# Chunks 0 to 3 and the weight conversion in a written order, O3 in the next chunk, scans straight from the loads

## Chip, cores, metric

One Trainium2 chip, one NeuronCore of it. The metric is the device time of one execution in microseconds (us).

## What is computed

Three layers one after the other, on 4 sequences of 768 steps (3072 tokens of 320 numbers): a linear recurrence with 8 heads of 40, a dense MLP with ELU (the kernel and this text call it MoE1), and a mixture of 8 experts with a balanced gate (MoE2).

```python
# recurrence, for each batch and head: state is 40 x 40
for t in range(S):                       # S = 768
    y[t]  = r[t] @ state
    Sa    = state @ a[t]
    state = state * w[t] - outer(Sa, b[t]) + outer(v[t], k[t])
# MoE1: x is y as (3072, 320), w_in 320 x 2048, w_out 2048 x 320
h = x @ w_in
x = where(h > 0, h, exp(min(h, 0)) - 1) @ w_out
# MoE2: 8 experts, w1 320 x 1024, w2 1024 x 320; P from x @ w_gate,
#       exp, then 8 rounds of row and column normalisation
out = sum over e of P[:, e:e+1] * (relu(x @ w1[e]) @ w2[e])
```

## The kernel before

**The recurrence in chunks.** The 768 steps are cut into 24 chunks of 32. Within a chunk the steps are solved together for all 32 pairs of batch and head, by small matmuls and one triangular solve; the state Y goes from chunk to chunk. A chunk c consists of these pieces, each a function that is called by a token of an order list:

- `ldw`, `ldk`, `lu`, `lv`: loads on SP's queue of WA (w and a), KE (k and b), VU (v), and of rB and rO (r). Many tiles exist once (r1 pool), so a load waits for the last reader of the chunk before.
- `prep`: VectorE clamps w twice (L316, into `wr` reversed, L317, into `wq`), one scan for the products F (L320), a reciprocal, a second scan for xE (L326); GpSimd makes aE (L328) and multiplies KE twice by F (L337); ACT copies aE into aB. It is a generator of five steps.
- `E1`, `E2`: transposes of KE and xE on TensorE, each with an ACT copy. `E3`: matmuls of KE with aB, on VectorE a mask (L367, into Am), then four stores of Am to DRAM (Ad, L382). `LT`: Ad comes back in the layout of the solve (L390).
- `T`, in function `tsolve`: the triangular solve on VectorE, instruction pairs Tt and Wk (L420 and L422 with halves for chunks 0 to 5, 15 pairs; L429 and L436 after that, 31 pairs), for one or two chunks at a time. Then stores to DRAM (Td, L444) and loads back (TT, L448).
- `E4`: matmuls of Am with VU. `H1`: matmuls of aE with Yw (L465), and an ACT copy to RH. `H2`: matmuls of TT with RH (L494), ACT copies to VU; chunks 0 to 5 do it twice, with L484 and RH on VectorE (L485) between. `H3`: matmuls of KB with VU (L518), and Y on VectorE. `YW`: GpSimd makes Yw. `H4`: transposes of Yw, ACT copies to Ss. H1, H2, H3, YW are what one chunk waits for from the one before.
- `O1`: transposes of VU, copies to uE (ACT and VectorE). `O2`: matmuls with rB, a mask on VectorE (L367, into Gm). `O3a`: matmuls of rO with Ss (L566). `O3b`: matmuls with Gm (L577), on VectorE a product (L580), a GpSimd copy, and a store of the chunk's output to DRAM (yd). These use four PSUM banks in turn; O1 and O3 have banks 2 and 3, E2 and O2 bank 2, E3 and the transposes of xprep bank 3 (table "ps").

**MoE1 beside it.** A unit is one of 16 slices of the hidden size for one of 12 blocks of 256 tokens (two chunks): 8 matmuls (L620), two ACT steps (L622, L623), g on VectorE (L629), gh on ACT, gl on GpSimd (L633), and 8 matmuls (L647 to L651) two units later. A token `m` advances by half a unit; `x` and `xl` advance `xprep`, which transposes a block of outputs (L603) and splits it on ACT and VectorE (L608). Before units can run their weights must be converted: 32 conversions (`w_in_split`, `w_out_split`), each a load of 320 to 384 KB, three VectorE instructions on the bits (L204 to L206), one on ACT, two on GpSimd.

**Order.** From chunk 4 on (`"fixed": 4`) each engine but SP runs its instructions in the order in which the lists "order" and "order2" (chunks below 6) call them: `pin_since` ties each instruction to the one before it on its engine. A `+3` means the piece of chunk c+3; a token `p` advances a running solve by three instructions, `G` lets it begin to be pumped. For chunks 0 to 3 the list "start" gives the pieces of chunks 0 and 1 and some of 2 to 5, and the lists go on at c = 2; but there the order on each engine is chosen by the scheduler, by priorities. The conversions are called in three groups (`w_5`, `w_5`, `w_22`). The solves of chunks 2 and 3 run singly, in the tokens `u` and `t`. SP's queue is ordered by the scheduler throughout.

**MoE2.** After chunk 23 and the last units of MoE1, `phase_b` runs 8 experts over 6 blocks of 512 tokens, in units of 128 hidden columns: `mm1` (L856), a split on ACT and VectorE (L859, L860), `mm2` (L899 to L901), and at the end of a block an accumulation (L910). Weights are loaded 11 units ahead. A range check reads w again at its side, and the output is stored per 128 tokens.

## Time and profile before

| | us |
|---|---|
| median of 3 runs | 2272.39 |
| the runs | 2266.86 to 2277.91 |
| the profiled execution | 2277.48 |
| its span, first to last instruction | 2275.6 |
| TensorE busy | 2146.8 (94%) |
| VectorE busy | 947.0 (42%) |
| ACT busy | 808.4 (36%) |
| GpSimd busy | 469.5 (21%) |

The profile calls the engines PE (TensorE, with PEld for its weight loads), DVE (VectorE), ACT, POOL (GpSimd) and SP. A busy share is an average over the whole span; the rows below give it by stretch. PEclk is the granted TensorE clock as a share of full speed. A wait is the idle time of an engine just ahead of an instruction, with the work whose end is thought to have released it; where an instruction waits for several, the one that came last by the profile is named.

### The profile page before, as it was taken

The numbers are of one execution on the slowest core, as the hardware profiler recorded it, in microseconds if no ns is written. First come the engines' busy times: TensorE is split into PE (matmuls) and PEld (weight loads), VectorE is DVE, ScalarE is ACT, GpSimd is POOL, SyncE is SP. The second block draws the span as 40 slices with busy tenths as digits, with TensorE's granted clock in tenths as the row PEclk, the third lists the DMA queues.
The fourth block names the chain that finished last, engine by engine and source line by source line (L and its number), as shares of the span: only waits on it lengthen the run. The fifth ranks groups of instructions, "written<-read, shape, count | busy, mean of one in ns | idle before, by whom it ended". The sixth has DMA issues, their size and how long they took to land.

```text
span 2275.6 us, 48283 instructions
## 1 busy us (share of the span) xinstructions
PE 2146.8 (94%) x20483; PEld 1931.9 (85%) x20483; DVE 947.0 (42%) x1963; ACT 808.4 (36%) x1789; POOL 469.5 (21%) x553
## 2 busy tenths in 40 slices
PE   2478999999999999999999999999999999999998
PEld 2367889888898989898888888888888888888887
DVE  7774777766666622532222222222222222222222
ACT  2243455544555555323324324223223212112111
POOL 5442344434343244002002002002002002001000
PEclk9998899999999999999999999999999999999999
DMA  6544344334443232101002012002002001000000
GB/s 169 151 116 116 91 112 109 102 100 102 107 105 78 60 90 84 45 1 55 19 20 71 21 32 77 26 26 77 26 26 70 1 1 52 1 1 20 24 24 25
DMA packets 179234, 138.34 MB, mean 61 GB/s; under 512 B 103873, under 2 KB 152386, under 8 KB 179010
## 3 DMA queue, kind: packets, MB, share of 16 engines
q1 hardware_dynamic: 179010, 135.17, 21.5%
q8 instruction: 162, 2.65, 0.5%
q14 instruction: 62, 0.51, 0.1%
HBM read 116.63 MB, written 18.48 MB: 59 GB/s over the span
## 4 chain that ended last, share of the span: by engine, by line
PE 75%; DVE 10%; DMA 7%; SPq 3%; issue 2%; ACT 1%; POOL 1%; DVEq 0%; ACTq 0%; POOLq 0%
PE h L856 28%; PE pa L900 10%; PE pa L901 10%; PE pa L899 10%; PE ph L620 4%; PE h L845 2%; DVE Wk L436 2%; DMA LT<-Ad 2%; PE a L647 2%; DVE Tt L429 1%; DMA WA<-in_wa 1%; PE a L648 1%; PE a L649 1%; SPq L448 1%; DMA Ad<-Am 1%
## 5 line engine op out<-in xcount | busy, mean ns | idle before, releaser
L860 DVE SCALAR_TENSOR_TENSOR hl<-h,hh 128x512 fp32r<-128x512 f32 x384 | 265.2, 691 | 765.9 <-ACT hh L859 765.4
L859 ACT ACTIVATE hh<-h 128x512 fp32r<-128x512 f32 x384 | 229.3, 598 | 899.7 <-PE h L856 899.2
L856 PE MATMUL h<-xs,a 128*128 128x512 f32 x2280 | 546.8, 394 | 0.0
L856 PEld LDWEIGHTS h<-xs,a 128*128 128x128 f32 x2280 | 421.1, 188 | 109.1 <-issue 25.4
L899 PE MATMUL pa<-a,hh 128*128 128x320 f32 x1536 | 474.0, 309 | 1.8 <-ACT acc L906 1.6
L900 PE MATMUL pa<-a,hl 128*128 128x320 f32 x1536 | 475.4, 310 | 0.0
L901 PE MATMUL pa<-a,hh 128*128 128x320 f32 x1536 | 475.2, 309 | 0.0
L899 PEld LDWEIGHTS pa<-a,hh 128*128 128x128 f32 x1536 | 288.8, 188 | 7.1 <-ACT acc L906 1.8
L900 PEld LDWEIGHTS pa<-a,hl 128*128 128x128 f32 x1536 | 288.9, 188 | 5.0 <-issue 0.2
L901 PEld LDWEIGHTS pa<-a,hh 128*128 128x128 f32 x1536 | 289.0, 188 | 0.0
L807 POOL TENSOR_TENSOR a<-rw,a 128x384 fp32r<-128x384 f32 x64 | 65.4, 1022 | 1055.3 <-ACT a L805 1046.4
L633 POOL TENSOR_TENSOR gl<-g,gh 128x256 fp32r<-128x256 f32 x192 | 162.5, 846 | 410.6 <-ACT gh L631 296.0
L620 PE MATMUL ph<-X,Wt 128*128 128x256 f32 x1536 | 237.3, 299 | 0.6 <-DVE g L629 0.5
L620 PEld LDWEIGHTS ph<-X,Wt 128*128 128x128 f32 x1536 | 206.3, 199 | 5.1 <-DVE g L629 1.0
L910 DVE SCALAR_TENSOR_TENSOR acc<-pa,Pg,acc 128x320 f32<-128x320 f32 x168 | 80.9, 545 | 184.5 <-PE pa L901 184.5
L629 DVE SCALAR_TENSOR_TENSOR g<-m,ph 128x256 f32<-128x256 f32 x192 | 80.2, 418 | 181.3 <-ACT m L623 164.5
L622 ACT ACTIVATE m<-ph 128x256 f32<-128x256 f32 x192 | 73.5, 383 | 176.7 <-PE ph L620 168.6
L631 ACT ACTIVATE gh<-g 128x256 fp32r<-128x256 f32 x192 | 80.0, 417 | 124.9 <-DVE g L629 123.8
L436 DVE TENSOR_TENSOR Wk<-Wk,Tt 128x132 f32<-128x132 f32 (+24 forms) x279 | 119.2, 427 | 6.5
L856 PE MATMUL h<-X,a 128*128 128x512 f32 x456 | 109.1, 394 | 0.6 <-DVE X L608 0.6
L856 PEld LDWEIGHTS h<-X,a 128*128 128x128 f32 x456 | 84.0, 188 | 22.6 <-issue 5.0
L429 DVE TENSOR_TENSOR Tt<-Wk,LT 128x132 f32<-128x132 f32 (+24 forms) x279 | 92.2, 330 | 19.6 <-DMA LT<-Ad 11.7
(183 smaller groups left out, 2713.0 us busy)
## 6 DMA issues: line engine op xcount, KB each, us to landing
LT<-Ad SPq DMA_DIRECT2D x24, 512.0 KB
rw<-in_moe_w SPq DMA_DIRECT2D x64, 160.0 KB
WA<-in_wa SPq DMA_DIRECT2D x24, 416.0 KB
KE<-in_kb SPq DMA_DIRECT2D x24, 416.0 KB
...
```

The source lines that it names most:

```text
L429: V.tensor_tensor(out=tv, in0=Wk[:, :, 0:ni, j:j + 1].to_broadcast(sh), in1=LT2[:, :, j, j + 1:C].unsqueeze(2).to_broadcast(sh), op=ALU.mult,)
L436: dve["T"] = V.tensor_tensor(out=Wk[:, :, 0:ni, j + 1:C], in0=Wk[:, :, 0:ni, j + 1:C], in1=tv, op=ALU.subtract)
L620: T.matmul(ph, lhsT=Wt[0:kp, wi, 128 * f:128 * f + 128], rhs=X[0:kp, xi, :], start=(i == 0), stop=(i == 7))
L629: V.scalar_tensor_tensor(out=g, in0=m, scalar=-1.0, in1=ph, op0=ALU.add, op1=ALU.max)
L633: G.tensor_tensor(out=gl, in0=g, in1=gh.bitcast(F32), op=ALU.subtract)
L856: T.matmul(h, lhsT=a1[:, wi, :], rhs=X[bk][:, xi, :], start=(i == 0 and n == 8), stop=(i == n - 1), skip_group_check=(n == 7))
L859: dve["hh"] = A.activation(out=hh, in_=h, func=AF.Relu)
L860: V.scalar_tensor_tensor(out=hl, in0=h, scalar=0.0, in1=hh.bitcast(F32), op0=ALU.max, op1=ALU.subtract)
L899: T.matmul(o, lhsT=hh[:, ts_], rhs=a2[:, 0, :], start=(f == 0), stop=False)
L900: T.matmul(o, lhsT=hl[:, ts_], rhs=a2[:, 0, :], start=False, stop=False)
L901: T.matmul(o, lhsT=hh[:, ts_], rhs=a2[:, 1, :], start=False, stop=(f == NF2 - 1))
L910: V.scalar_tensor_tensor(out=at, in0=o, scalar=Pg[:, tt, e:e + 1], in1=at, op0=ALU.mult, op1=ALU.add)
```

## The change

It changes four things.

1. **Chunks 0 to 3 and the 32 conversions** get a written order on all engines but SP. The new list START holds their pieces one step at a time, with the conversions in three tokens (`d` load, `b` bits on VectorE, `o` ACT and GpSimd), 11 units of MoE1 (`m`), and the solves in pairs, chunks 2 and 3 together (`u` begins one, `s_10` runs ten steps). All of it is pinned. The lists "order" and "order2" now begin at c = 4. For chunks 0 and 1, aE and the products of KE move from GpSimd to VectorE. The LT tiles of chunks 2 and 3 and chunk 1's loads share a tile (`two`).
2. **O3a and O3b** of chunk c stand at the top of chunk c+1 (`+-1`), O3b's matmuls first, then E4, O3a, H1. Which of O3a and O3b starts and ends the accumulation is decided by which comes first.
3. **E3** of chunk c+3 stands behind H2 instead of ahead of H1; LT moves with it.
4. **The scans** read w from the loaded tile: the host puts a zero ahead of each row of 32, the first scan runs backwards over it. The two clamps and their tiles go; xE has rows of 33, so ACT copies it into a dense tile xC for the transposes of E2. The range check skips the zeros.

Besides, the last four units of MoE2 run their second matmuls for the first two token tiles of all four units, then for the other two.

```diff
+START = """
+lu_0 prep_0*5 E3_0 ldw_2 E3_0 LT_0 E1_0 E2_0 prep_1*5 E3_1*2 LT_1 ldk_2 E4_0 H1_0 E1_1 E2_1 lu_1 d*2 lv_0 b o u_0_1 d b o prep_2 d prep_2*2 ldw_3 b
+s_10 s_11 b prep_2 s_10 o d prep_2 E3_2 b o E3_2 LT_2 E2_2 ldk_3 H2_0 o E1_2 prep_3*2 d*2 H2_0 prep_3 H2_0 O1_0 H3_0 prep_3*2 E3_3 b H3_0 o O1_0 d
+E3_3 YW_1 ldw_4 b E4_1 LT_3 O2_0 H1_1 E1_3 prep_4 ldk_4 E2_3 u_2_3 b o d O2_0 s_10 O3b_0 d lu_2 o H2_1 O3a_0 O3b_0 s_10 H2_1 s_10 prep_4 H2_1 prep_4
+ldw_5 H3_1*2 b o d O1_1*2 H4_1 lv_1 YW_2 O2_1 E4_2 prep_4*2 E3_4 b O3a_1 d O2_1 o prep_5 H1_2 O3b_1 b E3_4 LT_4 o O3b_1 s_9 E1_4 ldk_5 xl E2_4 d
+prep_5 H2_2 prep_5 x*2 b x*2 H2_2 prep_5 m prep_5 o ldw_6 b o d m H2_2 d E3_5 b m E2_5 E3_5 H3_2*2 E1_5 ldk_6 o d O1_2 prep_6*2 lu_3 m O1_2 H4_2 YW_3
+E4_3 m b o d u_4_5 prep_6 H1_3 lv_2 b O2_2 ldw_7 m o O2_2 d LT_5 H2_3 b o d s_10 m H2_3 O3a_2 b o d m O3b_2*2 H2_3 prep_6*2 b prep_7 ldw_8 d o H3_3 m
+E3_6 H3_3 b o d m E3_6 E2_6 E1_6 ldk_7 m b d o LT_6 s_10 prep_7 O1_3 H4_3 lu_4 b YW_4 m d o O1_3 b o lv_3 O2_3 b o d m O2_3 prep_7 b o d m O3a_3 b
+O3b_3 s_20 d b o m d m prep_7 b m o prep_7 m*2 O3b_3 d m o d m x b o b d m x b d o*2 x*2 b o
+"""
...
-    "order": "T lv E4 m p E3+3 xl m E3+3 p H1 m p E2+3 LT+3 m p H2 lu+1 m prep+4 p E1+3 ldk+4 m prep+4 p x m prep+4 p H3 m G x H3 p O1 m O1 p H4 m YW+1 prep+4 p O2 ldw+5 x m O2 p m x p O3a m prep+4 p O3b m O3b p m p m p w",
+    "order": "T O3b+-1 E4 p O3a+-1 H1 lv m p O3b+-1 m lu+1 m p H2 E3+3 xl m E3+3 p p m p E2+3 LT+3 m prep+4 E1+3 ldk+4 m prep+4 p x m prep+4 p H3 m H3 G x p O1 m O1 p H4 m prep+4 YW+1 p O2 m ldw+5 x O2 p m x p m prep+4 p m p m p",
+    "order2": "T O3b+-1 E4 m p O3a+-1 H1 lv m O3b+-1 p xl m p H2 lu+1 m prep+4 p H2 m prep+4 p H2 E3+3 m E3+3 E2+3 LT+3 prep+4 p H3 E1+3 ldk+4 x x m G H3 p O1 m O1 p H4 m YW+1 prep+4 p O2 ldw+5 x m O2 p m x p m prep+4 p m p m p m p",
-    "start": "prep_0 E3_0 LT_0 prep_1 E3_1 LT_1 E1_0 E2_0 lu_0 E1_1 w_5 E2_1 lu_1 E4_0 H1_0 ld_2 prep_2 E3_2 LT_2 lv_0 E1_2 T_0_1 u_2 w_5 ld_3 E2_2 H2_0 t_2 u_3 H3_0 O1_0 O2_0 O3a_0 O3b_0 E4_1 YW_1 H1_1 H2_1 O1_1 w_22 lu_2 ld_4 prep_3 H4_1 lv_1 O2_1 O3a_1 O3b_1 xl H3_1 YW_2 E3_3 LT_3 t_3 E2_3 E1_3 prep_4 E3_4 LT_4 E2_4 E1_4 ld_5 prep_5 ldw_6",
+    "start": START,
...
-    "fixed": 4,
+    "queue": False,
...
+    ws = np.concatenate([np.zeros_like(e["w"][..., :1]), e["w"]], -1).reshape(N, 2, D, -1)
+    out["wa"] = lay(np.concatenate([ws, np.zeros_like(ws[..., :1]), e["a"].reshape(N, 2, D, -1)], -1))
...
-        V.tensor_scalar(out=wr[0:HR, :, 1:C + 1], in0=wv[:, :, ::-1], scalar1=WLO, scalar2=WHI, op0=ALU.max, op1=ALU.min)
-        V.tensor_scalar(out=wq[0:HR, :, 1:C], in0=wv[:, :, 0:C - 1], scalar1=WLO, scalar2=WHI, op0=ALU.max, op1=ALU.min)
+        V.tensor_tensor_scan(out=F[0:HR, 1:NW + 1][:, ::-1], data0=z.WA[0:HR, 1:NW + 1][:, ::-1], data1=flat(dr)[0:HR], initial=0.0, op0=ALU.mult, op1=ALU.add)
...
+        V.tensor_tensor_scan(out=flat(z.xE)[0:HR], data0=z.WA[0:HR, 0:NW], data1=flat(dq)[0:HR], initial=0.0, op0=ALU.mult, op1=ALU.add)
+        (V if c < 2 else G).tensor_tensor(out=z.aE[0:HR].rearrange("p g (b t) -> p (g b) t", t=C), in0=z.WA[0:HR, NW + 1:].rearrange("p (x t) -> p x t", t=C), in1=z.xE[0:HR, :, 0:C], op=ALU.mult)
...
+        A.copy(out=z.xC[0:HR].rearrange("p g (b t) -> p (g b) t", t=C), in_=z.xE[0:HR, :, 0:C])
...
+        s, z.begun = not hasattr(z, "begun"), True
...
-                SY.dma_start(out=raw[0:rows], in_=wa_d[x][:, 0:size] if n == "w" else wp_d[x] if n == "i" else wo_d[x * 128:(x + 1) * 128, :])
+                SY.dma_start(out=raw[0:rows], in_=wa_d[x][:, 0:NW].rearrange("p (x t) -> p x t", t=C + 1)[:, :, 1:] if n == "w" else wp_d[x] if n == "i" else wo_d[x * 128:(x + 1) * 128, :])
...
+                seq += [(mm2, x + (p,)) for p in (range(0, TB // 2), range(TB // 2, TB)) for x in u]
```

## Rows read from the trace of the kernel before

**Rows 1.** Busy us by stretch: PE, PEld, DVE, ACT, POOL; PEclk, DMA share, GB/s
```profile
0.00:126.00 126.00, 51.99 (x809) 42.27 (x809) 91.81 (x190) 33.84 (x72) 64.38 (x85) 1.00 0.57 158
...
126.00:217.00 91.00, 78.76 (x1316) 70.36 (x1317) 53.55 (x124) 36.69 (x88) 35.74 (x43) 0.87 0.47 120
...
217.00:290.00 73.00, 67.63 (x1230) 63.03 (x1227) 45.32 (x107) 33.32 (x82) 22.80 (x29) 0.86 0.33 84
...
290.00:800.00 510.00, 485.53 (x8482) 455.72 (x8482) 351.26 (x831) 263.96 (x673) 198.79 (x229) 0.97 0.38 97
...
905.00:2276.00 1371.00, 1361.80 (x7630) 1205.00 (x7629) 380.10 (x660) 379.02 (x722) 99.37 (x106) 1.00 0.10 32
```

**Rows 2.** Timeline, chunks 0 to 3: start, us, engine, line, operation, [idle before <-releaser]
```profile
25.88 1.98 PE L365 MATMUL P<-aB,KE 104*64 104x64 f32 x32 [0.18 <-ACT aB L453]
...
33.79 1.16 DVE L367 TENSOR_TENSOR Am<-P,cst 128x1024 f32<-128x1024 f32 x1
...
45.36 0.22 DVE L420 TENSOR_TENSOR Tt<-Wk,LT 128x60 f32<-128x60 f32 x1 [8.87 <-DMA WA<-in_wa]
...
67.69 1.93 PE L494 MATMUL P<-RH,TT 64*64 64x40 f32 x32
...
111.11 1.93 PE L494 MATMUL P<-RH,TT 64*64 64x40 f32 x32 [1.78 <-DVE RH L485]
...
163.35 1.13 PE L494 MATMUL P<-RH,TT 64*64 64x40 f32 x32
...
213.07 0.55 PE L398 MATMUL P<-VU,Am 128*64 128x40 f32 x12
```

**Rows 3.** Groups by line on DVE, 0 to 217 us: busy, mean ns | idle before
```profile
L205 DVE SCALAR_TENSOR_TENSOR tmp<-raw,tmp 128x384 int32<-128x384 int32 (+1 forms) x32 | 21.5, 675 | 0.5
...
L206 DVE SCALAR_TENSOR_TENSOR tmp<-raw,tmp 128x384 int32<-128x384 int32 (+1 forms) x32 | 20.1, 632 | 0.6
...
L420 DVE TENSOR_TENSOR Tt<-Wk,LT 128x48 f32<-128x48 f32 (+19 forms) x60 | 19.5, 325 | 22.4 <-DMA LT<-Ad 8.9 <-DMA WA<-in_wa 8.9 <-DMA Wk<-in_consts 3.4
...
L204 DVE TENSOR_SCALAR tmp<-raw 128x384 int32<-128x384 int32 (+1 forms) x32 | 12.5, 392 | 16.9 <-DMA raw<-in_wp 7.3 <-DMA raw<-in_moe_w_out 4.5 <-POOL yt L581 1.9
...
L320 DVE TENSOR_TENSOR_SCAN F<-wr,dr 104x528 f32<-104x528 f32 x8 | 9.9, 1246 | 0.0
...
L317 DVE TENSOR_SCALAR wq<-WA 104x496 f32<-104x496 f32 x8 | 3.8, 477 | 0.0
...
L316 DVE TENSOR_SCALAR wr<-WA 104x512 f32<-104x512 f32 x8 | 3.4, 423 | 6.1 <-DMA WA<-in_wa 6.1
```

**Rows 4.** Timeline of DVE, one conversion instruction of chunk 0's stretch
```profile
20.77 2.30 DVE L205 SCALAR_TENSOR_TENSOR tmp<-raw,tmp 128x384 int32<-128x384 int32 x1
```

**Rows 5.** Group of O3a on PE, 290 to 800 us; then timeline of chunk 7
```profile
L566 PE MATMUL P<-Ss,rO 40*32 40x40 f32 x1024 | 14.9, 206 | 19.4 <-ACT m L623 12.2 <-DVE X L608 6.5 <-ACT m L622 0.5
...
338.58 1.12 PE L620 MATMUL ph<-X,Wt 128*128 128x256 f32 x8
...
339.64 1.22 DVE L367 TENSOR_TENSOR Gm<-P,cst 128x1024 f32<-128x1024 f32 x1
...
340.96 0.78 PE L566 MATMUL P<-Ss,rO 40*32 40x40 f32 x64 [1.26 <-ACT m L623]
```

**Rows 6.** Busy us by stretch, columns as in the first group, in chunk 12
```profile
490.00:500.00 10.00, 8.33 (x123) 7.64 (x123) 6.66 (x19) 2.11 (x6) 4.04 (x5) 0.66 0.22 59
```

**Rows 7.** Timeline of SP's queue and DVE around one solve's end, chunks 9 and 10
```profile
402.40 4.94 SPq L444 DMA_DIRECT2D Td<-Wk  x6
...
407.56 1.91 SPq L448 DMA_DIRECT2D TT<-Td  x4
...
410.79 1.22 DVE L367 TENSOR_TENSOR Am<-P,cst 128x1024 f32<-128x1024 f32 x1 [1.94 <-DMA TT<-Td]
...
415.99 1.91 SPq L382 DMA_DIRECT2D Ad<-Am  x4
...
424.29 0.22 DVE L429 TENSOR_TENSOR Tt<-Wk,LT 128x62 f32<-128x62 f32 x1 [1.12 <-DMA LT<-Ad]
```

More of the change, by code (lines that the diff above doesn't have):

```diff
@@ new lines, in conv, with tokens @@
+            if i < len(wgen):
+                conv_load(*wgen[i]) if n == "d" else (conv_bits if n == "b" else conv_out)(convs[i])
+                cvn[n] += 1
+                if n == "o" and i + 1 == len(wgen):
+                    cvx.close()
+                    late.append(moe.enter_context(tc.tile_pool(name="late", bufs=1)))
+        def tokens(x):
+            for t in x.split():
+                t, k = (t + "*1").split("*")[:2]
+                yield from [t] * int(k)
+        first_ins = traced()[-1]
```

220 lines of the change are left out of this document (104 added, 116 removed), and 3 rows, old and new, of the table PLAN.

## The prediction

> **What bounds the kernel now.** I read the busy time by stretch first [rows 1]. From 905 us to the end TensorE is busy for 1361.8 of 1371 us at a granted clock of 1.00: the second mixture of experts (MoE2) is limited by TensorE alone, and the change touches only its last four units. Everything else lies before 905. From 0 to 126 us TensorE works for 52.0 us and VectorE for 91.8; from 126 to 217 they work for 78.8 and 53.6, at a mean clock of 0.87. At about 217 the chunk loop reaches chunk 4, whose first matmuls, E4, stand at 213.07 [rows 2]. From 290 to 800 TensorE is busy for 485.5 of 510 us at 0.97. So time can be won in two places: up to 217, where 86 us of TensorE are idle and a chain through all engines is the limit, and from 217 to 800, where TensorE is nearly full and some 30 us are idle, with a clock that falls now and then.
>
> The work is conserved. By the tokens of the order lists, before has finished 12 units of the first MoE when chunk 3 ends and after has finished 11; from then on both do the same number in each chunk (8 from chunk 5 on). So what is won early is won at the end too, less one unit: 16 matmuls of 256 columns, 1.9 us (eight stand in 1.12 us with the last one's drain [rows 5], 0.96 a half unit without it).
>
> **Part 1: chunks 0 to 3 in fixed order.** When does chunk 4's E4 start, before at 213.1? The steps of before [rows 2]: E3 of chunk 0 at 25.9, the solve of chunks 0 and 1 from 45.4, H2 of chunk 0 at 67.7, the second H2 of chunk 1 at 111.1, of chunk 2 at 163.4.
>
> *To the solve.* After, VectorE does two memsets fewer and then chunk 0 alone. WA lands near 5 us; then a scan of 1.25 [rows 3], a reciprocal, the other scan, aE and both KE products, which are now on VectorE (0.63 each, by the two-source L206 [rows 3], 1.9 together), with two ACT copies beside them: E3 of chunk 0 near 10, its mask done near 13. Chunk 1 repeats it, and its mask ends near 21, before at 35.0 [rows 2]. From there before takes 10.4 us until the solve starts (Ad store, LT load), so it starts near 31 instead of 45.4. Conversions and scans of chunk 2 (8 us) fill most of the wait.
>
> *To H2 of chunk 1.* From the start of the solve to H2 of chunk 0 before takes 22.3 us, of which some 3.5 are other VectorE work that now stands elsewhere: H2 near 50. Behind it VectorE waits for matmuls (8.6 us until RH, 5 us until Y); Y ends near 65, and H1 of chunk 1 near 71, behind E3 of chunk 3, E4 and O2. The next 20 solve steps (chunks 2 and 3 in one solve) stand ahead of chunk 1's RH on VectorE and wait for the LT of chunk 3, whose mask ends near 67: 67 + 10.4 = 78. RH is then ready near 85, and so is the second H2 of chunk 1 (before 111.1).
>
> *To chunk 4.* From chunk 1 to chunk 2 the second H2 takes before 52 us, to chunk 4's E4 another 50. After, H1 of chunk 2 stands behind E3 of chunk 4, which waits for GpSimd's KE products, near 104; the second H2 of chunk 2 is near 119, of chunk 3 near 153. Behind that VectorE still has 36 us of its list (13 conversions at 1.7, 30 solve steps, a mask, seven g): chunk 4 begins near 187.
>
> A second count for that end: VectorE is busy for 145.4 us up to 217 [rows 1]. The change takes away the two clamps of eight chunks (7.2 us), a quarter of the 120 solve instructions, since chunks 2 and 3 become one solve (60 are L420, 19.5 us: 9.7 with the others), and memsets (1), and adds 3.8 for chunks 0 and 1 [rows 3]: 131 us are left. My chain holds some 50 us of waits (31 up to 85 us, about 20 later): 181. I take 187, 26 us earlier, less 1.9 for the unit: **24 us**. Bounds: with half of these waits 156 (55 us); with all of before's 72 us of idle time 203 (8 us). The ACT copy from xE to xC is new, 0.4 to 0.7 us a chunk by the clamps of as many elements [rows 3], hidden: ACT is half idle, and E2 has units to spare; without that cover it costs up to 24 x 0.7 = 17 us. A reversed read cost the clamp L316 nothing against the forward L317 [rows 3]; a scan's reversed write is not in the trace: from nothing to a doubling, 1.25 us a chunk, hidden in the loop, up to 5 us here. I take nothing.
>
> A conversion costs VectorE 1.7 us (54.1 us for 32 [rows 3]). Single two-source instructions are long where GpSimd works: L205, 0.68 in the mean, took 2.30 at 20.77 [rows 4]. After, a conversion's bits often run beside the last one's GpSimd subtractions. If each of the 64 took 1.3, 42 us would be added; I take the mean of before, which holds such cases. The Trainium skill (GPSIMD Engine Reference, 1. Specifications) says that GpSimd's SBUF interfaces are shared with VectorE and contended by instructions with two SBUF inputs; the trace agrees. By that rule the denser start goes towards the 42 us, by the rows of before towards none.
>
> **Part 2: chunks 4 to 23.** From 290 to 800 TensorE idles for 19.4 us ahead of L566, O3a [rows 5]. The profile names ACT m and the X subtraction; but in chunk 7 the mask Gm runs from 339.64 to 340.86 and O3a starts at 340.96, after 1.26 us of idle time: O3a writes the bank that Gm reads, half a unit behind it, and in chunks with an xprep the bank that X reads too. After, O3b comes first, over three half units later at the top of the next chunk, and then O3a: Gm is done by then. I count 18.7 us, those named by m and X. E4 and H1 simply follow; Am, VU and Yw are made long before.
>
> The clock: behind such a wait in chunk 12 the granted clock is 0.66 from 490 to 500 us [rows 6]. At the lower level of 1.2 GHz for 6.8 of these 10 us, TensorE loses 3.4. The 510 us lose 0.03 x 510 = 15 in this way [rows 1], nearly all in four such places. I take 13.6; if the falls stay, 0.
>
> What is late next? E3 now stands behind H2, and H2 waits for TT. Before, in chunk 10: Td is issued at 402.40, right behind the solve; TT at 407.56; the mask ends at 412.0, but its Ad store is issued only at 415.99, behind SP's other transfers; the next solve starts at 424.29, waiting for LT [rows 7]: 21.9 us. After: TT there 9.3 us behind the solve (409.5 and 2 to land, an estimate), H2 1.1, E3 1.2, half a unit and the mask 2.2, Ad and LT 8.3: 22.1, about the same. The solve is spread over 20 half units and some 15 us of the chunks' own matmuls, 34.6. Together that is 57 us for a pair of chunks, while TensorE needs 32 x 0.96 + 2 x 14 = 59 (14 an estimate: what is left of a chunk). It holds, by 2 us. H2 before has eight half units and six groups of matmuls, about 13 us, between the solve's end and its turn; after six and four, 8.8 to 9.8: a wait of up to 1 us in each of nine pairs, 3 with a delayed Td. I take **minus 4 us** (0 to minus 27). The later yd store costs nothing in the loop (six half units ahead of its reader) and up to 2 us once, in the last chunk; I count it in that range.
>
> From 217 to 290, 5.4 us are idle and 0.14 x 73 = 10 are lost to the clock [rows 1], part of it behind O3a: **6 us** (0 to 15). Loop: 18.7 + 13.6 - 4 = **28 us** (8 to 33).
>
> **Part 3, the rest.** With the last group's second matmuls in two halves, two accumulations instead of four are left behind the last matmul: under 0.5 us. The range check reads w in rows of 128 bytes instead of 2 KB, 24 times, while the DMA engines are a tenth busy [rows 1] and weights are loaded 11 units ahead: nothing.
>
> **Sum.** 24 + 6 + 28 = 58 us off the profiled execution's 2277.5, whose span is 2275.6: 2219. That execution was near the slowest of the four (2266.9 to 2277.9); off the median of 2272.4 it gives 2214. I say **2216**, between them and nearer the median.
>
> **Rivals.** (a) *The start wins little* (0.15): a fixed order stalls at its first late operand, and VectorE has its 72 idle us again. Start 8, total 42: 2232. For it: one late LT holds VectorE's whole list. Against: before pays the same wait, 8.9 us of it [rows 3]. (b) *Contention in the start* (0.05): 64 two-source instructions at 1.3 us put chunk 4 at 229, start minus 18, total 16: 2257. For it: the 2.30. Against: the mean of 0.68. (c) *The loop keeps its period* (0.16): new waits for TT, or a clock that still falls, leave 8 us of the loop: 2236. For it: 9.3 against 8.8 to 9.8. (d) *The start is bound by the recurrence alone* (0.14): chunk 4 begins near 165: 2194. (e) *Slower* (0.05): the solve's loop through DMA becomes the limit. Place: SP's queue, where the mask's Ad stands behind loads that now wait longer (rO behind the later O3a, yt behind the later yd). Each us by which that delays Ad beyond 2 is lost in each of ten pairs; at 8 the gain is gone, at 10 it gives 2292. Before, the delay was 4 us and came from TT, which is issued by then. (f) *Nothing changes* (0.04), as the scheduler's order was as good: 2270.
>
> **How the numbers follow.** The forecast has 0.41. The range leaves out no more than 0.2: it reaches over (a), (c) and (d) with their bounds, 2188 to 2250. About 0.5% (11 us) is what a measurement of this kernel can tell from no change. Faster: the forecast and (a) to (d), some of (b) aside: 0.88. Same, with (f): 0.06. Slower: 0.06.
>
> **What would show it.** Right: E3 of chunk 0 near 10, the solve from 31, the second H2 of chunk 1 near 85, chunk 4 near 187; no idle time ahead of O3a or O3b, and a clock of 1.00 from 300 to 750. Wrong: chunk 4 after 205; TensorE waiting at H2 for TT, or VectorE for LT above 3 us a pair; dips of the clock in the old places.

## The result, and the profile after

The changed kernel takes 2243.67 us (median; 2241.65 to 2252.16), the kernel before, run beside it, 2273.93 (2266.86 to 2277.91): a ratio of 0.9877 with an interval of 0.9841 to 0.9914. That is 30 us less, where 58 were forecast, and it lies inside the forecast's range of 2188 to 2250. The profiled execution is the one of 2241.65, its span 2239.8.

Busy time by stretch of the changed kernel (columns as in [rows 1], which it answers):

```profile
0.00:126.00 126.00, 68.73 (x1308) 60.70 (x1309) 82.79 (x160) 41.89 (x92) 41.39 (x60) 0.84 0.59 156
126.00:217.00 91.00, 69.49 (x1149) 63.62 (x1147) 64.33 (x122) 38.65 (x95) 45.02 (x64) 0.77 0.51 139
217.00:290.00 73.00, 68.08 (x1204) 64.35 (x1203) 52.69 (x120) 39.22 (x98) 27.01 (x31) 0.95 0.42 106
290.00:800.00 510.00, 485.36 (x8718) 463.14 (x8717) 346.26 (x791) 274.12 (x700) 201.00 (x235) 0.98 0.37 94
905.00:2239.00 1334.00, 1328.85 (x7444) 1175.15 (x7442) 360.76 (x620) 364.52 (x699) 99.41 (x106) 1.00 0.11 30
```

The stretch of MoE2 is as full as it was. Up to 126 us TensorE does 68.7 us of work instead of 52.0. But from 290 to 800 it is busy for 485.4 of 510 us, against 485.5 in [rows 1]: the 24 idle us of the loop are all still there.

The timeline of the changed kernel at the steps of [rows 2] (start, us, engine, line, operation, idle time before and its releaser; L383 is E3, for other tiles also O2, L436 the solve, L510 H2, L416 E4; a row stops where the stretch that was asked for stops, so it can show fewer matmuls than the group has):

```profile
11.21 1.97 PE L383 MATMUL P<-aB,KE 104*64 104x64 f32 x32 [11.21 <-ACT aB L469]
...
31.94 0.22 DVE L436 TENSOR_TENSOR Tt<-Wk,LT 128x60 f32<-128x60 f32 x1
...
50.37 0.41 PE L510 MATMUL P<-RH,TT 64*64 64x40 f32 x2 [10.46 <-DMA TT<-Td]
...
84.70 0.55 PE L510 MATMUL P<-RH,TT 64*64 64x40 f32 x6 [8.00 <-DVE RH L501]
...
116.88 0.33 PE L510 MATMUL P<-RH,TT 64*64 64x40 f32 x2
...
143.46 0.36 PE L510 MATMUL P<-RH,TT 64*64 64x40 f32 x5
...
188.44 0.44 PE L416 MATMUL P<-VU,Am 128*64 128x40 f32 x4
```

E3 of chunk 0 stands at 11.2, the solve starts at 31.9 (45.4 in [rows 2]), H2 of chunk 0 is at 50.4 (67.7), the second H2 of chunk 1 at 84.7 (111.1), of chunk 2 at 116.9 (163.4), of chunk 3 at 143.5, and E4 of chunk 4 at 188.4 (213.1): 24.6 us earlier.

The group of O3a, 290 to 800 us, of the changed kernel (columns as in [rows 5]):

```profile
L583 PE MATMUL P<-Ss,rO 40*32 40x40 f32 x1152 | 14.3, 200 | 0.0
```

Its 19.4 us of idle time [rows 5] are gone. In their place, in the view of TensorE's waits over the same stretch (what waited, for whom: us in all, times, longest):

```profile
PE P L383 <- issue: 5.7, 4, 1.7
PE P L481 <- issue: 5.7, 6, 1.6
PE P L365 <- ACT xT L469: 4.1, 6, 0.9
PE P L510 <- DMA TT<-Td: 2.5, 7, 0.7
PE ph L638 <- DVE g L647: 1.8, 6, 0.5
```

E3 (L383) and H1 (L481) wait, E1 (L365) waits for a copy of ACT, H2 for TT, MoE1 for g. "issue" means that the view names no releaser. Together with some smaller ones that makes 24.6 us again. From E4 of chunk 6 to E4 of chunk 23 the changed kernel takes 511.3 us, the profiled execution of before 521.6. Those 10 us and the start's 24.6 are 35 of the 35.8 us between the two profiled executions; whether the 10 belong to the change is the first question.

### The profile page after: what moved, and what is told of

It reads as the page before. It is cut to its first block, busy times and chain, and to the rows that moved or that the text cites. A ratio compares the mean times of both kernels' runs of the same rounds, so it can differ in the third digit from the quotient of the medians.

```text
span 2239.8 us, 48166 instructions
## 1 busy us (share of the span) xinstructions
PE 2120.8 (95%) x20483; PEld 1920.2 (86%) x20483; DVE 942.9 (42%) x1889; ACT 816.7 (36%) x1813; POOL 453.6 (20%) x545
## 4 chain that ended last, share of the span: by engine, by line
PE 73%; DVE 14%; DMA 6%; SPq 3%; issue 2%; ACT 1%; POOL 0%; DVEq 0%; ACTq 0%; POOLq 0%
PE h L874 28%; PE pa L918 10%; PE pa L919 10%; PE pa L917 10%; DVE Wk L452 4%; PE ph L638 4%; DVE Tt L445 3%; PE h L863 2%; DMA LT<-Ad 2%; DVE g L647 1%; PE P L383 1%; PE P L510 1%; SPq L460 1%; PE a L665 1%; SPq L464 1%
## 5 line engine op out<-in xcount | busy, mean ns | idle before, releaser
L649 ACT ACTIVATE gh<-g 128x256 fp32r<-128x256 f32 x192 | 80.0, 416 | 163.4 <-DVE g L647 162.5
L445 DVE TENSOR_TENSOR Tt<-Wk,LT 128x132 f32<-128x132 f32 (+24 forms) x279 | 100.6, 361 | 24.3 <-DMA LT<-Ad 16.2
```

Of the source, the lines that this page charges most:

```text
L445: V.tensor_tensor(out=tv, in0=Wk[:, :, 0:ni, j:j + 1].to_broadcast(sh), in1=LT2[:, :, j, j + 1:C].unsqueeze(2).to_broadcast(sh), op=ALU.mult,)
```

## Experiments

Times are medians; each ratio is to the kernel before, run on the same chip at the same time, with its 95% interval. "6 to 23" is the time from E4 of chunk 6 to E4 of chunk 23.

### The parts one by one

**start_only**: in the changed kernel, the lists of before.

```diff
-    "order": "T O3b+-1 E4 p O3a+-1 H1 lv m p O3b+-1 m lu+1 m p H2 E3+3 xl m E3+3 ...
+    "order": "T lv E4 m p E3+3 xl m E3+3 p H1 m p E2+3 LT+3 m p H2 ... x m O2 p m x p O3a m prep+4 p O3b m O3b p m p m p",
```

> The changed kernel with the loop lists of before from chunk 4 on (O3 at the chunk's end, E3 ahead of H1). The fixed order of chunks 0 to 3 and the scans stay. Theory: the start is worth 24.6 us (chunk 4's E4 at 188.4 instead of 213.1) whatever loop follows; E4 of chunk 4 near 188, TensorE's waits ahead of O3a back (15 to 20 us from chunk 4 to 23), time 20 to 25 us below before (ratio 0.989 to 0.991), so 6 to 11 us above the changed kernel. Rival 1, the lists of the loop carry the gain and the start's lead is given back at chunks 4 and 5: less than 10 us below before. Rival 2, the new loop gains nothing: as fast as the changed kernel (ratio 0.987).

Measured: 2244.45, ratio 0.9852 (0.9811 to 0.9892); the changed kernel has 2243.67. E4 of chunk 4, from its timeline, and the group of O3a, 290 to 800 us:

```profile
187.61 0.98 PE L416 MATMUL P<-VU,Am 128*64 128x40 f32 x14
```

```profile
L583 PE MATMUL P<-Ss,rO 40*32 40x40 f32 x1088 | 15.0, 201 | 8.5 <-DVE X L626 8.5
```

Rival 2 holds: the start with the scans is worth the whole change, and the new lists add nothing on top that the medians show. From 6 to 23 it takes 512.3 us, as the changed kernel does (511.3), although O3a still waits for 8.5 us.

**loop_only**: in the kernel before, the new lists from chunk 4 on (with O3a and O3b in either order).

```diff
-            for n, o in orders[c < PLAN["halves"]]:
+            for n, o in orders[(c < PLAN["halves"]) + (c < 4)]:
```

> The kernel before with the new loop lists from chunk 4 on (O3 in the next chunk, E3 behind H2); its start, its clamps and its scans stay. Theory: chunk 4's E4 stays at 213; the waits ahead of O3a go, new ones of the same size come ahead of E3 and within H1, the granted clock falls less often; time 6 to 13 us below before (ratio 0.994 to 0.997). Rival 1 (the prediction): 28 to 34 us below before (0.985 to 0.988). Rival 2: nothing or slower, as the two clamps that stay (0.9 us of VectorE per chunk) delay O3b's product further: 0.998 to 1.005.

Measured: 2266.51, ratio 0.9979 (0.9959 to 1.0000): 6 us, the theory's lower end, at the edge of what can be told from nothing. One place is clear: from E4 of chunk 4 to that of chunk 5 it takes 33.7 us, before 39.5; but chunk 5 then takes 35.9, before 33.7, so that 3.5 of these 5.8 us are left at chunk 6. From 6 to 23 it takes 514.5.

**scan_only**: in the kernel before, part 4 of the change alone.

```diff
-        V.tensor_scalar(out=wr[0:HR, :, 1:C + 1], in0=wv[:, :, ::-1], ...
-        V.tensor_scalar(out=wq[0:HR, :, 1:C], in0=wv[:, :, 0:C - 1], ...
+        V.tensor_tensor_scan(out=F[0:HR, 1:NW + 1][:, ::-1], data0=z.WA[0:HR, 1:NW + 1][:, ::-1], ...
...
+        A.copy(out=z.xC[0:HR].rearrange("p g (b t) -> p (g b) t", t=C), in_=z.xE[0:HR, :, 0:C])
```

> The kernel before with the scans of the change alone (w with zeros between its rows, no clamps, xE copied into xC by ACT, range check that skips the zeros); start and loop lists of before. With the start alone the loop of before took 587.8 us from chunk 4's E4 to chunk 23's instead of 594.8, and its waits ahead of O3a fell from 19.4 to 9.0 us, those behind the mask Gm to none. Theory: this is the scans: without the two clamps VectorE reaches Gm 0.9 us earlier in each chunk. Then this kernel has 8 to 11 us of waits ahead of O3a between 290 and 800 us, none behind ACT m, and is 4 to 9 us below before (ratio 0.996 to 0.998). Rival: the scans do nothing (the prediction took nothing for the loop): 18 to 20 us ahead of O3a, ratio 0.999 to 1.001, and the 7 us are the start's or a difference between executions.

Measured: 2269.0, ratio 0.9996 (0.9978 to 1.0014). The rival holds: two clamps less per chunk and one ACT copy more are worth nothing that the medians show. Chunk 4's E4 does come earlier, at 203.5 instead of 213.1, but chunks 4 and 5 then take 79.2 us instead of 73.1. The run says more, though. O3a's group and the stretch from 290 to 800 us:

```profile
L565 PE MATMUL P<-Ss,rO 40*32 40x40 f32 x1088 | 14.9, 200 | 18.2 <-ACT m L622 8.8 <-DVE X L607 6.6 <-ACT m L621 2.8
```

```profile
290.00:800.00 510.00, 488.26 (x8666) 458.31 (x8664) 346.51 (x808) 276.59 (x700) 195.31 (x235) 0.99 0.38 98
```

O3a waits for 18.2 us as before, 6 to 23 takes 511.4 us, and the granted clock is 0.99, where [rows 1] has 0.97. So the old lists can run the loop as fast as the changed kernel does, with O3a's waits. The 10 us by which the profiled execution of before was slower there lie in four of its solves (a stretch runs from a solve's start to its end), such as this one:

```profile
485.65:527.35 41.70, 38.39 (x654) 35.93 (x653) 35.18 (x88) 20.78 (x53) 16.41 (x18) 0.92 0.37 97
```

These four have a granted clock of 0.92 and take 41.6 to 41.8 us each; the three ahead of them, at 1.00, take 38.8 to 39.7. scan_only has one such solve (0.92, 41.8 us), although O3a waits as long. The 10 us thus come from more falls of the clock in that one execution, and O3a's waits do not carry these falls with them.

**start_gps**: aE and the products of KE of chunks 0 and 1 back on GpSimd.

```diff
-            (V if c < 2 else G).tensor_tensor(out=kv[:, :, kb, :], ...
+            G.tensor_tensor(out=kv[:, :, kb, :], ...
```

> The changed kernel with aE and the products of KE of chunks 0 and 1 on GpSimd, as before. The prediction took the solve's start (31 instead of 45) from chunk 0 being taken first and from these products on VectorE. Theory: each product takes 1.25 us on GpSimd instead of some 0.65 on VectorE, with a change of engine: E3 of chunk 0 and 1 later by 2 to 4 us, the solve from 34 to 36 instead of 31.9, chunk 4's E4 2 to 4 us later than 188.4. Rival: VectorE is the limit up to 85 us and gains as much as GpSimd's part costs: solve and E4 as before within 1 us.

Measured (one execution, 2248.11): a product takes 1.18 us on GpSimd, 0.68 on VectorE. E3 of chunk 0 stands at 11.4 instead of 11.2, of chunk 1 at 21.1 instead of 19.3, the solve at 33.6 instead of 31.9, but E4 of chunk 4 at 188.0, where the other kernels with this start lie between 185.7 and 189.5. The theory holds for the first steps, with less than the 2 to 4 us that it said, and the rival for the end: of these 1.7 us nothing is left at chunk 4.

### Taking the new waits away

**h1_apart**: half a unit ahead of H1 (and E4 behind O3a).

```diff
-"T O3b+-1 E4 p O3a+-1 H1 lv m p O3b+-1 ...
+"T O3b+-1 p O3a+-1 E4 m H1 lv p O3b+-1 ...
```

What H1's waits look like in the changed kernel, chunk 16 (timeline, PE):

```profile
567.44 0.79 PE L583 MATMUL P<-Ss,rO 40*32 40x40 f32 x64
...
568.04 0.90 PE L481 MATMUL P<-Yw,aE 40*32 40x40 f32 x62
...
570.52 0.34 PE L481 MATMUL P<-Yw,aE 40*32 40x40 f32 x2 [1.57 <-issue]
```

62 of 64 matmuls run, then TensorE stands still for 1.57 us in the middle of one group, and two more follow; the view names no releaser. In the next five chunks the same happens behind 58, 48, 44, 34 and 30 matmuls.

> The changed kernel, order from chunk 6 on: O3b O3a E4, then half a unit of MoE1, then H1 (O3b E4 O3a H1 stood back to back: 192 matmuls of 30 ns or less and as many weight loads). Theory: the six waits in the middle of H1 (5.7 us, chunks 16 to 21, behind 62, 58, 48, 44, 34 and 30 of its 64 matmuls) are TensorE waiting for its own instructions: when 256 instructions pass in less than some 2.4 to 3.1 us the next ones are not there. With half a unit between, 256 instructions take 3 us: the waits in H1 fall below 1 us, the clock falls behind them go, time 6 to 12 us below the changed kernel (ratio to before 0.982 to 0.985). Rival: they are a wait for another engine (Yw, RH's bank): they stay within H1 at 5 to 6 us, time as the changed kernel (0.987).

Measured: 2238.58, ratio 0.9842 (0.9812 to 0.9872), 5 us below the changed kernel and within what can't be told from it. H1's group, 290 to 800 us:

```profile
L481 PE MATMUL P<-Yw,aE 40*32 40x40 f32 x1088 | 14.0, 201 | 0.0
```

The waits in H1 are gone, as expected if TensorE waited for its own instructions there. 6 to 23 takes 507.6 us: of 5.7 us some 4 are kept at most, and E3 and O2 (for uE) wait for longer instead (8.8 us together, 7.1 before the move).

**product_first** and **e3_bank0**: E3's wait. In chunk 9 E3 starts at 360.28, behind 1.71 us of idle time; O3b's product on VectorE, which reads the same bank, runs from 359.63 to 360.18. The first kernel moves the product ahead of six solve instructions, the second E3 to another bank.

```diff
-E4 p O3a+-1 H1 lv m p O3b+-1 m lu+1
+E4 O3a+-1 H1 lv m O3b+-1 p p m lu+1
```

> The changed kernel, order from chunk 6 on: O3b's product on VectorE ahead of the two groups of three solve instructions that stood before it at the chunk's top. Theory: E3's waits of 1.7 us in chunks 9, 11 and 13 (5.7 us in all) are for this product, which reads the bank that E3 writes and stands behind solve instructions on VectorE: they fall below 1.5 us in all, the clock falls behind them too, time 5 to 12 us below the changed kernel (ratio to before 0.982 to 0.985). Rival 1: VectorE is behind by its whole list there, and the product is as late as before: 4 to 6 us of waits stay, same time. Rival 2: the solve's last steps come later and TensorE waits at H2 for TT instead: 5 us more at H2, same time.

```diff
-        yield from masked(PS["E3"][0], HR, ...
+        yield from masked(bank[0] if c >= 9 else PS["E3"][0], HR, ...
```

> The changed kernel with E3 of chunks 9 and later in PSUM bank 0, which no one reads between RH's copy and H3, instead of bank 3, which O3b's product on VectorE reads. Theory: E3's waits of 1.7 us are for that bank alone: none is left ahead of E3 in chunks 6 to 23 (5.7 us before), without delaying anything else; the waits within H1 stay (5 to 7 us); time 3 to 8 us below the changed kernel (ratio to before 0.984 to 0.987). Rival: VectorE, not the bank, is late there: the mask of E3, LT or uE then make TensorE wait elsewhere for as long, and the time stays at 0.987 to 0.989.

Measured: 2249.52, ratio 0.9892 (0.9860 to 0.9924), and 2250.62, ratio 0.9915 (0.9882 to 0.9947). Neither gains. The waits of e3_bank0, 260 to 800 us:

```profile
PE a L665 <- ACT x L672: 7.9, 7, 2.0
PE P L481 <- issue: 5.6, 6, 1.5
PE P L365 <- ACT xT L469: 5.3, 7, 0.9
```

E3's waits for the product are gone in both, so the bank was their cause. But MoE1 (L665) now waits for ACT's copies, 7.9 us against 1.1. The rivals hold: a wait removed here returns there.

**three_waits**: h1_apart, e3_bank0, and E1 half a unit later.

```diff
-... E2+3 LT+3 m prep+4 E1+3 ldk+4 m prep+4 p x m ...
+... E2+3 LT+3 m prep+4 m E1+3 ldk+4 prep+4 p x m ...
```

> The changed kernel with three moves from chunk 6 on: half a unit between O3b O3a E4 and H1 (as in h1_apart), E3 in bank 0 (as in e3_bank0), and E1 half a unit further behind E2. Theory: the loop's new waits (E3 5.7, H1 5.7, E1 4.1 us) each have their own cause and add up: all three are gone, 8 to 10 us are idle from chunk 6 to 23 instead of 24, the clock is at 0.99 or above, time 10 to 20 us below the changed kernel (ratio to before 0.979 to 0.983). Rival: VectorE and the solve's loop through DMA hold the pace behind these waits (waits for uE, TT, LT take their place): 20 us stay idle, time within 5 us of the changed kernel (0.985 to 0.988).

Measured: 2240.21, ratio 0.9859 (0.9826 to 0.9892); 6 to 23 takes 509.0 us. H1's waits fell to 1.0 us, E3's and E1's are gone, and from 260 to 800 us TensorE is idle for 26.8 us, at other lines (26.0 in the changed kernel). The rival holds.

**o3a_later**: start_only with O3a half a unit later, nothing else.

```diff
-O2 p m x p O3a m prep+4 p O3b m O3b p m p m p
+O2 p m x p m O3a prep+4 p O3b m O3b p m p m p
```

> The new start and scans with the loop lists of before, in which O3a alone stands half a unit later (behind the unit that followed it). Question: what is O3a's wait worth by itself? With the start and the old lists TensorE waited 9.0 us ahead of O3a between 260 and 800 us and 21 us in all. Theory 1 (as the prediction had it): the wait is a loss of its own; 0 to 2 us are left ahead of O3a, 12 us idle in all, time 8 to 14 us below the start with the old lists (2244.5), ratio to before 0.979 to 0.983. Theory 2 (a pace set elsewhere): other waits grow by as much, 18 to 24 us stay idle, ratio 0.984 to 0.988.

Measured: 2240.13, ratio 0.9866 (0.9826 to 0.9906). O3a waits for 3.3 us instead of 8.5, and MoE1's first matmuls for g 13.1 instead of 6.5: theory 2. With the old lists, too, this wait is no loss of its own that the medians show (2244.45 with it). The profiled executions alone would say otherwise: from 6 to 23 this one takes 500.8 us, at a granted clock of 1.00, 11.5 us less than start_only's. But its chunks 4 and 5 take 78.3 us against 75.5, and its four times reach from 2230.88 to 2247.08, start_only's from 2232.42 to 2246.82: how much of the 11.5 us is the move's, one execution can't tell.

### What sets the pace

These five kernels gave next to nothing, so I asked what a pair of chunks takes, from the start of one solve to the start of the next. Busy time in the solve's own stretch and in the gap behind it, of the changed kernel (chunks 8 to 12) and of before (chunks 10 to 12):

```profile
343.39:381.50 38.11, 36.10 (x596) 34.68 (x595) 36.39 (x86) 21.34 (x55) 16.34 (x18) 0.96 0.37 100
381.50:403.62 22.12, 21.86 (x444) 20.71 (x443) 8.12 (x16) 11.46 (x29) 9.29 (x11) 1.00 0.54 119
403.62:441.70 38.08, 34.92 (x594) 33.19 (x594) 36.36 (x86) 21.36 (x55) 16.32 (x18) 1.00 0.38 101
441.70:464.04 22.34, 21.79 (x443) 20.57 (x442) 8.15 (x17) 11.55 (x29) 9.28 (x11) 1.00 0.51 118
```

```profile
424.29:463.10 38.81, 36.09 (x659) 33.78 (x658) 36.22 (x88) 20.98 (x54) 16.57 (x18) 1.00 0.37 103
463.10:485.65 22.55, 22.32 (x385) 21.00 (x385) 8.80 (x18) 11.35 (x29) 9.05 (x11) 1.00 0.43 108
```

While a solve runs, VectorE is busy for 36.4 of 38.1 us (36.2 of 38.8 before). Between solves it is busy for 8.1 of 22.1. Over 510 us this makes 69% [rows 1], and that hides it. (The pair of before is one with a granted clock of 1.00; the four solves at 0.92 have 35.2 to 35.4 us of VectorE in 41.6 to 41.8.) In the gap TensorE is full, 21.9 of 22.1 us; what the next solve waits for at its end is LT, behind the transfers on SP's queue; it answers [rows 7]:

```profile
381.33 0.18 DVE L452 TENSOR_TENSOR Wk<-Wk,Tt 128x16 f32<-128x16 f32 x1
...
381.55 3.85 SPq L460 DMA_DIRECT2D Td<-Wk  x6
...
390.95 2.66 SPq L464 DMA_DIRECT2D TT<-Td  x4
...
392.03 1.23 DVE L385 TENSOR_TENSOR Am<-P,cst 128x1024 f32<-128x1024 f32 x1 [1.27 <-PE P L383]
...
395.12 1.85 SPq L400 DMA_DIRECT2D Ad<-Am  x4
...
398.22 0.56 SPq L408 DMA_DIRECT2D LT<-Ad  x1
...
403.62 0.23 DVE L445 TENSOR_TENSOR Tt<-Wk,LT 128x62 f32<-128x62 f32 x1 [2.29 <-DMA LT<-Ad]
```

The solve ends at 381.5. Td goes out, TT, the rest of Td and of TT; E3's mask is done at 393.3, Ad is issued at 395.1 behind TT, LT at 398.2, and the next solve starts with its landing at 403.6: 22.1 us from Td's issue, where [rows 7] has 21.9. Followed in the same way, the gap is 21 to 25 us in the kernel before, start_only, h1_apart, three_waits, o3a_later and the changed one, whatever the order of O3, E3 and H1.

**e3_ahead_h2**: h1_apart with E3 ahead of H2 (in bank 0, as in e3_bank0), so that Ad can go earlier.

```diff
-... O3b+-1 m lu+1 m p H2 E3+3 xl m E3+3 p p m p E2+3 ...
+... O3b+-1 m E3+3 xl lu+1 m E3+3 p H2 m p p m p E2+3 ...
```

> The changed kernel with H1 apart (as in h1_apart) and, from chunk 6 on, E3 half a unit behind H1 and ahead of H2 (bank 0 for chunks 9 and later); O3 stays at the next chunk's top. Theory: behind H2 E3 closes a loop (solve, TT, H2, E3, LT, next solve); TensorE's waits move from place to place because this loop sets the pace. Taken out of it, VectorE's waits for LT fall from 14 us to below 5, TensorE idles for 10 to 15 us from chunk 6 to 23 instead of 20 (h1_apart), ratio to before 0.978 to 0.982. Rival: the loop has slack; LT earlier changes nothing, 18 to 24 us idle, ratio 0.983 to 0.987.

Measured: 2239.95, ratio 0.9864 (0.9840 to 0.9889). The mask ends 9.7 us behind the solve instead of 11.8, but Ad still stands behind TT on SP's queue, 13.7 us behind the solve, and the gap is 23.2 us. The experiment didn't do what it was for: LT came no earlier, VectorE waited for it for 17.4 us (14.0 in the changed kernel, 18.8 in h1_apart).

**solve_faster** and **solve_even**: h1_apart with four solve instructions per `p`, and the changed kernel with four in even chunks and three and two in turn in odd ones.

```diff
-    "tp": ((3, 3), (3, 3)),
+    "tp": ((4, 4), (4, 4)),
```

> h1_apart with four solve instructions per token p instead of three. Theory (the solve's loop sets the pace): the solve ends some 8 us earlier in each pair, waits for TT go, chunk 6 to 23 in 500 us or less instead of 507.6, ratio to before 0.979 to 0.983. Rival (VectorE's list sets it): with more solve instructions between two g, what TensorE and ACT want from VectorE comes later (uE, O3b's product, g); their waits grow by 5 to 15 us, ratio 0.986 to 0.992.

```diff
-    "tp": ((3, 3), (3, 3)),
+    "tp": ((4, 4), (3, 2)),
```

> The changed kernel with the solve's steps dealt out otherwise: four per token p in even chunks, three and two in turn in odd ones (three everywhere before). VectorE's work is the same and moves from odd to even chunks, some 5 us of it. Theory (odd chunks are VectorE's): odd chunks go from 31.7 to 29.5 us, even ones stay at 28.5; eight pairs give 10 to 16 us; ratio to before 0.980 to 0.983. Rival: the sum of the pair is what counts, or LT comes too late to use the even chunk: within 4 us of the changed kernel, 0.985 to 0.989.

Measured: 2266.95, ratio 0.9983 (0.9968 to 0.9998), and 2251.86, ratio 0.9920 (0.9896 to 0.9944). Solve and gap of solve_faster:

```profile
352.44:386.54 34.10, 31.22 (x529) 29.73 (x528) 32.19 (x80) 16.89 (x44) 12.99 (x15) 0.95 0.33 88
386.54:417.99 31.45, 30.20 (x533) 28.29 (x533) 11.49 (x23) 16.17 (x41) 11.54 (x14) 1.00 0.53 122
```

The solve is 4 us shorter than in h1_apart (38.1), the gap 8 longer (23.3): the next solve needs E3 and LT at their place in TensorE's list, and TensorE had fallen behind (E3 alone waits for 14.3 us). In solve_even the solve's stretch holds 35.2 us of VectorE in 38.7, and a pair 60.6 us, as without it. Work that is dealt out otherwise within the stretch stays in the stretch.

**solve_light** and **solve_light_old**: the changed kernel and start_only with half of the solve's instructions left out from chunk 6 on, so that half of it isn't computed.

```diff
+            if j % 2:
+                yield
+                yield
+                continue
             tv = tmp[:, 0:n * ni * nt].rearrange("p (x i t) -> p x i t", x=n, i=ni)
```

> The changed kernel with every second pair of solve instructions left out for chunks 6 and later (half the solve is not computed; the tokens p stay, each with three steps of which half are empty). VectorE was busy for 29.0 of 31.8 us in chunk 9 and 15.6 of 28.5 in chunk 10. Theory: in the odd chunks VectorE, not TensorE, sets the time, and TensorE's waits there (E3, uE, the later halves) are its shadow. Without half the solve (some 99 of 198 us between chunk 6 and 23) odd chunks take 29 us or less, 10 us or less are idle from chunk 6 to 23 apart from those within H1 (5.7), the stretch takes 490 to 500 us instead of 511; ratio to before 0.979 to 0.983. Rival (transfers set it: LT, TT): 20 us or more stay idle, 507 to 512 us, 0.985 to 0.989.

> The new start with the loop lists of before, and the same half of the solve left out for chunks 6 and later. If O3a's wait is a loss of its own (a bank that the mask or X reads, too near in the order), it stays at 9 us or more with VectorE relieved, and the new lists beat the old by 5 to 10 us here. If it is VectorE's lateness too, it goes below 4 us and both lists take the same, 490 to 500 us from chunk 6 to 23. Ratio to before 0.981 to 0.986 in the first case, 0.979 to 0.983 in the second.

Measured: 2210.18, ratio 0.9732 (0.9709 to 0.9756), and 2226.7, ratio 0.9807 (0.9782 to 0.9832). One pair of solve_light:

```profile
334.75:369.30 34.55, 34.26 (x598) 33.10 (x596) 26.67 (x55) 22.14 (x54) 15.99 (x17) 1.00 0.40 110
369.30:392.92 23.62, 23.56 (x461) 22.54 (x460) 8.28 (x16) 12.36 (x31) 10.06 (x12) 1.00 0.55 123
```

With VectorE at 26.7 us the solve's stretch falls to 34.6 us, the gap stays, TensorE is full in both, and four chunks (8 to 12) take 112.3 us, 56.2 per pair. 6 to 23 takes 482.4 us with the new lists and 492.5 with the old. Over seven pairs the mean is 57.2 us with the new lists, 58.4 with the old. So the solve's stretch is VectorE's, and the gain is larger than the theory said (490 to 500 us). The new order does have a gain, 16.5 us by the medians, once VectorE is out of the way; but waits are not what it saves: O3a waits for 4.6 us with the old lists, and TensorE is idle from 6 to 23 for 10.0 us with the new lists and 9.2 with the old. The 10 us of 6 to 23 lie in its busy time, 472.4 against 483.3 us for the same pieces; why these take longer was not tried.

**even_apart_act**: solve_even, h1_apart, and uE on ACT.

```diff
-... "UE": "AV", ...
+... "UE": "AA", ...
```

> solve_even and h1_apart together, and both copies of uE on ACT instead of one on VectorE (0.68 us per chunk). If VectorE in the odd chunks and the waits within H1 are the two losses of the new lists, they add up: 500 us or less from chunk 6 to 23, 15 us or less idle, ratio to before 0.976 to 0.981, below both kernels. Rival: ACT's part of the solve's stretch (VU, KB, aB, m) takes VectorE's place as the late one: 0.983 to 0.987.

Measured: 2239.21, ratio 0.9859 (0.9833 to 0.9885); 6 to 23 takes 509.3 us. E3 waits for 8.5 us, and O2 for uE from ACT 2.6. The rival's time.

**ad_act_e3** and **ad_act_old**: e3_ahead_h2 and o3a_later with Ad of the odd chunks from 9 on on ACT's queue, to shorten the gap.

```diff
-            SY.dma_start(out=Ad[bb * H:(bb + 1) * H]...
+            (A if c % 2 and c >= 9 else SY).dma_start(out=Ad[bb * H:(bb + 1) * H]...
```

> e3_ahead_h2 with the Ad stores of chunks 9, 11, 13 and so on issued on ACT's queue instead of SP's. In all kernels so far the next solve begins 21 to 25 us after the last one's end, whatever the order: Td, TT, Ad and LT go through SP's queue one after the other (in e3_ahead_h2 the mask of E3 ends 9.8 us behind the solve, Ad is issued 13.8 behind it, LT 17.1, the solve starts at 23.4); in the solve's own stretch VectorE is busy for 36.4 of 38.1 us. Theory: these two make a closed loop, 22 + 38 = 60 us per pair, and it sets the pace. Then Ad goes 3 to 4 us earlier, the gap is 19 to 21 us, a pair takes 57 to 58 us instead of 60, eight pairs give 12 to 25 us: ratio to before 0.976 to 0.981, chunk 6 to 23 in 485 to 497 us. Rival: TensorE and VectorE together set the pace, the gap merely fills what is left: the gap shrinks but the solve's stretch grows by as much; 0.984 to 0.988.

> The new start, the loop lists of before with O3a half a unit later (o3a_later), and Ad of the odd chunks on ACT's queue. There E3's mask ends 9.7 us behind the solve and Ad is issued 13 us behind it. Theory (closed loop): the gap falls from 21.5 by 2 to 4 us, the same 10 to 25 us are won: ratio to before 0.977 to 0.982. Rival: the gap shrinks and the solve's stretch grows, or ACT, waiting for the mask, delays m and gh: 0.985 to 0.990.

Measured: 2271.83, ratio 0.9994 (0.9978 to 1.0010), and 2263.79, ratio 0.9962 (0.9945 to 0.9979): 32 and 24 us above the kernels that they are built on. ACT's waits in ad_act_old:

```profile
ACT RH L469 <- DMA Ad<-Am: 32.6, 6, 6.2
```

```profile
397.13 4.37 ACTq L400 DMA_DIRECT2D Ad<-Am  x4
```

The second row is the four stores on ACT's queue: 4.37 us, on SP's 1.85. ACT stands at them for up to 6.2 us, RH and VU come late, and the gap grows to 23 to 28 us. Both theories' numbers are missed; a shorter gap wasn't reached.

**ad_twice**: instead, the gap lengthened, and nothing else: Ad issued twice.

```diff
+        if c % 2 and c >= 9:
+            Ad2 = drp.tile([B * H, C, C], F32, tag="Ad2", name="Ad2", bufs=3)
+            for bb in range(B):
+                ...
+                SY.dma_start(out=Ad2[bb * H:(bb + 1) * H]..., in_=z.Am[p0:p0 + C, u, :, C * bi:C * bi + C])
```

> The changed kernel with the four Ad stores of chunks 9, 11, ... 23 issued twice, first to a place that nobody reads, then to Ad: some 1.9 us more on SP's queue between the end of one solve and the start of the next, eight times; nothing else differs, on no queue. In the changed kernel the solve starts 22 to 24 us behind the last one's end and then takes 38.1 us, of which VectorE is busy for 36.4; a pair takes 60.2. Theory (a closed loop of solve and transfers, with no slack): each pair takes 1.5 to 2 us more, gap 24 to 26 us, solve's stretch the same 38; 11 to 16 us in all, 2255 to 2260 us, ratio to before 0.992 to 0.996. Rival (the gap is only what is left between two solves, TensorE and VectorE set the pace): the solve's stretch shortens by what the gap grows, or nothing grows; 2241 to 2247 us, 0.986 to 0.989.

Measured: 2260.96, ratio 0.9973 (0.9960 to 0.9987): 17 us above the changed kernel by the medians, 22 by the ratios, where 11 to 16 were expected. 6 to 23 takes 530.5 us, 19 more. Two pairs, and VectorE's wait for LT, 260 to 800 us:

```profile
349.19:387.40 38.21, 34.54 (x570) 33.23 (x571) 36.49 (x86) 21.32 (x55) 16.30 (x18) 0.96 0.31 87
387.40:412.05 24.65, 23.46 (x467) 22.05 (x465) 8.09 (x16) 11.44 (x29) 9.29 (x11) 1.00 0.54 130
412.05:450.10 38.05, 34.73 (x569) 33.23 (x570) 36.33 (x86) 21.53 (x55) 16.30 (x18) 0.96 0.32 90
450.10:476.85 26.75, 23.53 (x467) 22.11 (x465) 8.14 (x17) 11.44 (x29) 9.27 (x11) 1.00 0.55 126
```

```profile
DVE Tt L451 <- DMA LT<-Ad: 34.3, 7, 6.6
```

The gap grows from 22.1 and 22.3 to 24.7 and 26.8 us, the solve's stretch stays at 38.2 and 38.1, and VectorE waits for LT for 34.3 us instead of 14.0. The theory holds: the solve doesn't shorten by what the gap grows, so solve and transfers are one closed loop without slack, 38 + 22 = 60 us per pair, in the changed kernel. In the kernel before a pair at full clock takes as long by the rows above (38.8 + 22.6); that it is the same loop there was not tried.

## Why the prediction was half right

**Part 1** was right. The solve (31 said, 31.9 measured), H2 of chunk 0 (50, 50.4), the second H2 of chunks 1 and 2 (85, 84.7; 119, 116.9) and chunk 4's E4 (187, 188.4) agree. The last step was right by luck, as two errors cancel in it: the second H2 of chunk 3 came at 143.5 instead of 153, and from there VectorE's list took 45 us instead of 34. The second count fits as well: VectorE is busy for 133 us up to there (131 said) and waits for 55 (50). With start_only the start is shown to be worth 28 us by the medians (scans included, which alone give 0.7), 24 in the prediction. Rivals (a), (b) and (d) fall. Conversions did get dearer beside GpSimd, 1.92 us of VectorE instead of 1.70, 7 us over all of them, a sixth of the 42 of rival (b): the first of their two-source instructions (L215) takes 1.04 us in the mean where GpSimd works for more than half of it (14 of them), 0.54 in the other 18. The scan that now runs backwards takes 1249 ns (L336), forwards 1246 [rows 3]: nothing, as taken.

**Part 2, chunks 4 and 5**: 6 us were said. loop_only has 5.8 of them in chunk 4 and 3.5 over both chunks; in the changed kernel the two take 72.4 us against 73.1 of before, 0.7 less. In chunk 4 its H2 waits 4.3 us for RH from ACT, on which conversions of the start's list stand ahead; that the gain went there was not tried.

**Part 2, the loop**, is the step that failed: 28 us said, none measured (2244.45 with the old lists, 2243.67 with the new). Three terms of it:

- *O3a's 18.7 us* went from their place, as the prediction said they would. That they are a gain took for granted that TensorE sets the pace around them. It doesn't: with them (scan_only) and without them 6 to 23 takes 511.4 and 511.3 us.
- *The solve's loop*, 22.1 us of transfers and 34.6 of solve. The first is right (22.1 in the rows above). The second is the mis-sized term: 34.6 was how long TensorE needs for the work beside the solve, but VectorE needs longer for its own, 36.4 busy in 38.1 us. With that the loop is 60 us, not 57. solve_light bears this out: with VectorE relieved the stretch takes the 34.6 us. The other side, TensorE's 59 us per pair, was too high: solve_light shows 56.2 to 57.2. "It holds, by 2 us" was wrong by about 6, and in the other direction. Rival (c) came nearest to the outcome (2236; 2243.67 measured) and named "new waits for TT", which were 2.5 us, or a clock that still falls, which it does; the mechanism, a solve that VectorE fills and that LT ties to the next one, none of the rivals had. Rival (e) named this loop, as a risk of the change.
- *The clock's 13.6 us* were read from one execution, of which [rows 6] is a part, with more falls than that of scan_only, which keeps O3a's waits and has 0.99 from 290 to 800 us; the changed kernel has 0.98 without them, not the 1.00 that was forecast. In its loop a fall costs nothing that can be seen: the solve's stretch takes 38.11 us at 0.96 and 38.08 at 1.00 (rows above).

The lost unit and part 3 can't be seen: from E4 of chunk 23 to the end both kernels take 1468 us.

What stays open: a shorter gap, with Ad ahead of TT on SP's queue, wasn't reached by any of these kernels, so that it would win time is made likely by ad_twice but is not shown, and TensorE, too, is full in the gap (21.9 of 22.1 us). h1_apart, even_apart_act, e3_ahead_h2, o3a_later and three_waits lie 3 to 5 us below the changed kernel, each within what can't be told from it.
